# A branch on TensorE per step in a mixture-of-experts stage: 192 or 128 slots per expert

## The chip, the core and the metric

The kernel runs on one core of one Trainium2 chip. Its time is the device time of one execution in microseconds (us). TensorE multiplies matrices out of SBUF into PSUM, and each of its matmuls needs a weight load of its own; ScalarE (ACT in the rows), VectorE (DVE) and GpSimd (POOL) work on tiles; SyncE (SP) issues most transfers. Each engine has its own program and waits for the others through semaphores.

## The reference

Three stages follow each other: a sparse attention, a dense feed-forward layer with SiLU, and a routed layer with eight experts. Only the last is touched here:

```python
logits = x @ w_gate                      # x: 1152 tokens x 512
expert_idx = np.argmax(logits, axis=1)   # one expert per token
...
for i in range(N):                       # token i takes the next slot of its expert
    e = expert_idx[i]
    if counts[e] < capacity:             # capacity 288
        disp[e, counts[e]] = x[i]
        ...
h = np.maximum(np.einsum('ecd,edf->ecf', disp, w1), 0.0)   # 512 -> 1024, relu
y = np.einsum('ecf,efd->ecd', h, w2)                       # 1024 -> 512
out[i] = gate_w[i] * y[expert_idx[i], pos[i]]
```

How many tokens an expert gets depends on the data. With the inputs that `setup_inputs()` draws by default (seed 0), the reference's own counts are 138, 114, 113, 171, 190, 182, 128 and 116 tokens for experts 0 to 7.

## The kernel before

Attention and the feed-forward layer fill the first part of the program; the change leaves them as they are, except for eight more columns in the table of constants. Near the end of the feed-forward layer the tokens are routed: for every expert the kernel makes lists of its tokens in slots (`idx_g` to gather, `idx_o` to scatter, `gate`), with an index out of bounds in a slot that has no token.

The expert stage gives every expert NW = 192 slots, as a first chunk of P = 128 and a second of N1 = 64. Slots beyond 192 (up to the capacity) are done in a second pass at the end, which all engines skip if no expert needs it (`tc.If(flags[0] > 0)`, L1132). `r_final` counts the tokens of each expert by a matmul with ones, compares with 192 and writes the number of experts above it to `flag_i`; `get_flags` (L1087) loads it into a register of each engine, in the first step of expert 3.

The work of one expert is eight steps i, each for 128 of the 1024 hidden columns. In step (e, i) TensorE does
- `up` (L1055): four fp32 matmuls over the four blocks of 128 input columns, 192 slots wide, into a PSUM bank `u` (three banks in turn). In the trace each has two weight loads and two matmuls, so eight of each a step.
- `down` (L1074 to L1077 and `mm3`, L161 to L163) for the step three earlier (LAG = 3): five matmuls of 512 columns in fp32r. Three go into bank `y` (the first 128 slots), two into bank `z` (the 64 others).

Behind that come the step's other jobs (`fills`): ScalarE and VectorE split w2 of the next expert into a high and a low part (L235, L236, steps 0, 2, 4 and 6), TensorE turns the next expert's gathered tokens (`prep`, L930, steps 5 and 6), SyncE loads w1 and w2 of later experts. Then `relu` (L1061 on ScalarE, L1063 on VectorE) makes the tile `ht` of this step, which `down` takes three steps later; the bank `u` is free again at the same moment. After an expert's last `down`, `put_out` weighs both chunks with the gate and scatters them (L1044 to L1048); slots without a token are dropped by the bounds check.

Each engine runs its program in the order written; TensorE's order in the stage is up(s), down(s - 3), transposes if any, up(s + 1). Nothing reorders it.

Of the kernel before, what the change touches and what calls it, by code (L numbers as in the profile page):

```python
# [1 line left out]

# [7 lines left out]
F32 = mybir.dt.float32  # L10
F32R = mybir.dt.float32r
I32 = mybir.dt.int32
# [3 lines left out]
ALU = mybir.AluOpType  # L16
AX = mybir.AxisListType

P = 128
# [5 lines left out]
PW = 384  # L25
N1 = 64
NW = P + N1
# [12 lines left out]
LAG = 3  # L40
# [2 lines left out]
_C = {}  # L43
_off = 0
for _name, _w in (("ident", 128), ("ml", KW), ("ml0", KW), ("ms", 54), ("tri", 128),
                  ("rev", 8), ("tok", 18), ("iota", PW)):
    _C[_name] = (_off, _w)
    _off += _w
CW = _off
# [3 lines left out]
def constants():  # L53
    c = np.zeros((P, CW), np.float32)

    def put(name, a):
        o, w = _C[name]
        c[: a.shape[0], o:o + w] = a

    i = np.arange(P)  # L60
    put("ident", np.eye(P))
    q = (i % QB)[:, None]
    col = np.arange(KW)[None, :]
    ok = (col > q) & (col <= q + STRIDE)
    put("ml", np.where(ok, 0.0, -8e9))
    put("ml0", np.where(ok & (col >= STRIDE), 0.0, -8e9))
    c54 = np.arange(54)[None, :]
    ok = (q // 18 == c54 // 18) & (c54 % 18 <= q % 18)
    put("ms", np.where(ok, 0.0, -8e9))
    put("tri", (i[:, None] < i[None, :]) * 1.0)  # L70
    put("rev", np.broadcast_to(8.0 - np.arange(8), (P, 8)))
    tok = np.empty((P, 9, 2))
    tok[:, :, 0] = i[:, None]
    tok[:, :, 1] = P * np.arange(9)[None, :]
    put("tok", tok.reshape(P, 18))
    slot = np.full(PW, -1.0)
    slot[0:NW] = np.arange(NW)
    slot[2 * P:PW - 32] = NW + np.arange(P - 32)
    put("iota", np.broadcast_to(slot, (P, PW)))
    return c  # L80
# [3 lines left out]
def tile_kernel(ctx, tc, cap, q, k, v, w_in, w_out, w_gate, w1, w2, consts, out):  # L84
    nc = tc.nc
# [3 lines left out]
    E, _, F = w1.shape  # L89
# [8 lines left out]
    cst = ctx.enter_context(tc.tile_pool(name="cst", bufs=1))  # L98
    dram = ctx.enter_context(tc.tile_pool(name="dram", bufs=1, space=bass.MemoryType.DRAM))
    rp = ctx.enter_context(tc.tile_pool(name="rp", bufs=3))  # L100
# [11 lines left out]
    def C(name):  # L112
        o, w = _C[name]
        return cs[:, o:o + w]
# [7 lines left out]
    idx_g = cst.tile([P, 3, E], I32, name="idx_g")  # L122
    idx_o = cst.tile([P, 3, E], I32, name="idx_o")
    gate = cst.tile([P, 3, E], F32, name="gate")
    flag_i = cst.tile([1, 1], I32, name="flag_i")
    x2d = dram.tile([NT, DM], F32, name="x2d")

    pp = ctx.enter_context(tc.tile_pool(name="ps", bufs=1, space=bass.MemoryType.PSUM))
# [5 lines left out]
    def psum(tag):  # L134
        name = rings[tag].pop(0)
        rings[tag].append(name)
        return pp.tile([P, 512], F32, tag=name, name=tag, bufs=1)
# [22 lines left out]
    def mm3(o, ah, al, bh, bl, first, last):  # L160
        nc.tensor.matmul(o, lhsT=ah, rhs=bh, start=first, stop=False)  # L161
        nc.tensor.matmul(o, lhsT=ah, rhs=bl, start=False, stop=False)  # L162
        nc.tensor.matmul(o, lhsT=al, rhs=bh, start=False, stop=last)  # L163
# [82 lines left out]
    def l1_mm(g, tb, c, tag):  # L246
        s, o = 2 * (g % 2), P * c
        hp = psum(tag)
        for kk in range(KC):
            mm3(hp[:, 0:TB], whi[s][:, kk, o:o + P], wlo[s][:, kk, o:o + P],  # L250
                xhi[:, kk, tb * TB:(tb + 1) * TB], xlo[:, kk, tb * TB:(tb + 1) * TB], kk == 0, kk == KC - 1)
            if kk < KC - 1:
                yield
        yield hp[:, 0:TB]
# [35 lines left out]
    def first_up():  # L290
        for c in range(2):
            for hp in l1_mm(0, 0, c, "f"):
                if hp is not None:
                    copies.append((nc.vector.tensor_copy if c else nc.scalar.copy, hb[c], hp))
                yield


    with ExitStack() as actx:
# [212 lines left out]
        up = first_up()  # L511
# [21 lines left out]
        for i in range(NGR):  # L533
# [6 lines left out]
            n, part = groups[i][:2]  # L540
# [21 lines left out]
        z = NGR - VL  # L562
        up = l1_mm(0, 0, 2, "f")
        transpose_p(z + 1, "h")
        values(z)
        copy_out()
        normalise(z + 3, z - 1)
        next(up)
        transpose_p(z + 2)
        values(z + 1)  # L570
# [3 lines left out]
        silu(0, 0, 1, hb[1])  # L574
        evacuate_lo(z)
        next(up)
        next(up)
        transpose_p(z + 3, "h")
        hp = next(up)
# [7 lines left out]
        up = l1_mm(0, 0, 3, "acc")  # L587
# [205 lines left out]
    def r_slot_ids(out, src):  # L793
        t = rp.tile([P, 3, E], F32, tag="fin", name="fin", bufs=1)
        t = t[:, 0:src.shape[1], 0:src.shape[3]]
        nc.vector.scalar_tensor_tensor(out=t, in0=src[:, :, 0], scalar=-OOB, in1=src[:, :, 1],
                                       op0=ALU.mult, op1=ALU.add)
        nc.vector.tensor_scalar(out, t, OOB, None, op0=ALU.add)

    def r_final():  # L800
        extra = ohs
        cp = psum("m")
        for j, o in enumerate([cum] + extra):
            nc.tensor.matmul(cp[:, 0:E], lhsT=ones, rhs=o, start=j == 0, stop=j == len(extra))
        f = rp.tile([1, E], F32, name="flag", bufs=1)
        nc.vector.tensor_scalar(f, cp[0:1, 0:E], float(NW), None, op0=ALU.is_gt)
        fs = rp.tile([1, 1], F32, name="flags", bufs=1)
        nc.vector.tensor_reduce(out=fs, in_=f, axis=AX.X, op=ALU.add)
        nc.vector.tensor_copy(flag_i, fs)
        r_slot_ids(idx_o, idx)  # L810
# [69 lines left out]
    for n in range(4, nseq - 4):  # L880
        g, tb, c = seq[n]
# [167 lines left out]
            out=out, out_offset=bass.IndirectOffsetOnAxis(ap=idx_o[:n, ch, e:e + 1], axis=0), in_=y[:n], in_offset=None,  # L1049
            bounds_check=NT - 1, oob_is_err=False)  # L1050

    def up(e, i, n=NW):
        hp = psum("u")
        for kk in range(KC):
            nc.tensor.matmul(hp[:, 0:n], lhsT=w1b[e % 3][:, kk, P * i:P * i + P], rhs=X[e % 2][:, kk, 0:n],  # L1055
                             start=kk == 0, stop=kk == KC - 1)
        return hp

    def relu(hp, parts, n=NW):
        t = ep.tile([P, 2 * NW], F32R, tag="ht", name="ht", bufs=LAG + 1)  # L1060
        nc.scalar.activation(out=t[:, 0:n], in_=hp[:, 0:n], func=AF.Relu)  # L1061
        for o, c, m in parts:
            nc.vector.scalar_tensor_tensor(out=t[:, o:o + m], in0=hp[:, c:c + m], scalar=0.0, in1=t[:, c:c + m],  # L1063
                                           op0=ALU.max, op1=ALU.subtract)
        return t

    def down(e, i, t, y0, y1):
        j, c = 2 * (e % 2) + i // 4, i % 4
        for y in ((y1, y0) if i == 7 else (y0, y1)):
            if y is y0:  # L1070
                mm3(y0, t[:, 0:P], t[:, 2 * P:3 * P], whi[j][:, c], wlo[j][:, c], i == 0, i == 7)
            else:
                if i < 7:
                    nc.tensor.matmul(y1, lhsT=t[:, P:2 * P], rhs=whi[j][:, c], start=i == 0, stop=False)  # L1074
                nc.tensor.matmul(y1[:N1], lhsT=t[:, P:NW], rhs=wlo[j][:, c], start=False, stop=False)
                if i == 7:
                    nc.tensor.matmul(y1, lhsT=t[:, P:2 * P], rhs=whi[j][:, c], start=False, stop=True)  # L1077
# [6 lines left out]
    flags = []  # L1084

    def get_flags():
        flags.append(nc.values_load(flag_i[0:1, 0:1], min_val=0, max_val=E))  # L1087

    fills = {}

    def fill(e, i, *fs):
        fills.setdefault((e, i), []).extend(fs)

    fill(0, 0, (r_match, BB))
    fill(0, 1, (r_index, BA))
    fill(0, 2, (r_index, BB), (gather, 1, 0), (gather, 1, 1), (r_final,))
    fill(0, 3, (r_weigh, BA))
    fill(0, 4, (r_weigh, BB))
    for e in range(E):
        fill(e, 3 if e == 0 else 0, (gather, e + 2, 0))  # L1100
        fill(e, 4 if e == 0 else 1, (gather, e + 2, 1))
        for h in range(4):
            fill(e, SPLIT_AT[h], (split, e + 1, h))
        fill(e, 5, (prep, e + 1, 0))
        fill(e, 6, (prep, e + 1, 1))
        for j in range(2):
            fill(e, 3 + 4 * j, (w1load, e + 3, j))
    fill(3, 0, (get_flags,))

    r_match(BA)  # L1110
    PARTS = ((NW, P, N1), (NW + N1, 0, P))
    ht, ys = {}, {}
    for s in range(8 * E + LAG):
        e, i = divmod(s, 8)
        if s < 8 * E:
            hp = up(e, i)
        d, c = divmod(s - LAG, 8)
        if s >= LAG:
            if c == 0:
                ys[d] = psum("y"), psum("z")  # L1120
            down(d, c, ht.pop((d, c)), *ys[d])
        for f, *args in fills.pop((e, i), []):
            f(*args)
        if s < 8 * E:
            ht[e, i] = relu(hp, PARTS)
        if s >= LAG and c == 7:
            y0, y1 = ys.pop(d)
            put_out(d, 1, y1)
            put_out(d, 0, y0)
    assert not fills, fills  # L1130

    with tc.If(flags[0] > 0):  # L1132
        n = ROWS[2]
        for e in range(E):
# [11 lines left out]
            for i in range(8):  # L1146
                t = relu(up(e, i, n), ((n, 0, n),), n)
                j, c = 2 * (e % 2) + i // 4, i % 4
# [32 lines left out]
```

## Time and profile before

| | us |
|---|---|
| three runs | 485.38, 490.08, 487.12 (median 487.12) |
| the profiled execution, its own time | 483.33 |
| span of the trace in it | 481.5 |
| expert stage, first to last matmul | 303.5 to 470.3 |
| from there to the end of the span | 11.2 |

The span is the time from the first to the last instruction in the trace; 1.8 us of the execution's time lie outside it. The rows further down name an engine, a line of the kernel, the operation, and the tiles as out<-in. PE stands for TensorE's matmuls, PEld for its weight loads, and a q behind an engine's name for what its sequencer does itself: waits, register loads, branches. The matmul's times overlap with the next one's, so its cost is the distance from one start to the next.

### The profile page before, as it was taken

How to read it: one execution, taken by the hardware profiler on the slowest of the kernel's cores; microseconds unless marked ns; L12 is line 12 of the kernel's file. 1: busy time of each engine (PE TensorE's matmuls, PEld its weight loads, DVE VectorE, ACT ScalarE, POOL GpSimd, SP SyncE). 2: the span in 40 equal slices, each digit the busy share in tenths (PEclk: the TensorE clock that was granted, in tenths of full speed). 3: DMA queues.
4: the chain of work that ended last, by engine and by line, in shares of the span. 5: the costliest groups of instructions: out<-in, count | busy, mean ns of one | idle time of the engine just before them, and what ended most of it. 6: DMA issues, size and time to landing. Idle time of an engine off the chain costs nothing. (4 is left out here: it accounts for less than half of the span.)

```text
span 481.5 us, 8430 instructions
## 1 busy us (share of the span) xinstructions
PE 455.1 (95%) x3053; PEld 390.3 (81%) x3055; DVE 285.5 (59%) x785; ACT 203.8 (42%) x521; POOL 120.5 (25%) x152
## 2 busy tenths in 40 slices
PE   8989898999998989999999999999999999999990
PEld 4667677898887879887998888988888888888880
DVE  3676999357878855787325686654454454455210
ACT  4576787245463432534244143323343342423211
POOL 1323553012332320323054215420220303101001
PEclk9987999999999999999999999799999999999996
DMA  7989747014243650446034013998767677200000
GB/s 158 217 211 231 179 144 241 29 44 132 87 132 96 211 176 0 138 169 219 0 88 152 3 67 114 372 305 286 244 200 225 232 247 232 76 1 31 1 23 24
DMA packets 52363, 69.04 MB, mean 143 GB/s; under 512 B 19800, under 2 KB 29272, under 8 KB 52316
## 3 DMA queue, kind: packets, MB, share of 16 engines
q1 hardware_dynamic: 50268, 63.18, 42.8%
q0 software_dynamic: 2048, 5.26, 3.6%
q8 instruction: 26, 0.43, 0.4%
q14 instruction: 21, 0.17, 0.1%
HBM read 61.60 MB, written 7.86 MB: 144 GB/s over the span
## 5 line engine op out<-in xcount | busy, mean ns | idle before, releaser
L1055 PE MATMUL u<-X,w1b 128*128 128x192 f32 x512 | 95.7, 331 | 0.0
L1055 PEld LDWEIGHTS u<-X,w1b 128*128 128x128 f32 x512 | 86.1, 192 | 6.3
L198 POOL TENSOR_TENSOR wlo<-w,whi 128x512 fp32r<-128x512 f32 x32 | 44.2, 1383 | 117.4 <-DVE gl L267 79.5
L1061 ACT ACTIVATE ht<-u 128x192 fp32r<-128x192 f32 x64 | 21.2, 331 | 105.0 <-PE u L1055 65.2
L161 PE MATMUL acc<-whi,gh 128*128 128x512 f32 x144 | 58.2, 404 | 4.7 <-DVE x L288 4.6
L161 PE MATMUL h<-xhi,whi 128*128 128x384 f32 x176 | 59.8, 340 | 0.0
L163 PE MATMUL h<-xhi,wlo 128*128 128x384 f32 x176 | 59.4, 338 | 0.0
L162 PE MATMUL h<-xlo,whi 128*128 128x384 f32 x176 | 59.4, 338 | 0.0
L163 PE MATMUL acc<-whi,gl 128*128 128x512 f32 x144 | 56.9, 395 | 0.0
L162 PE MATMUL acc<-wlo,gh 128*128 128x512 f32 x144 | 56.7, 394 | 0.0
L1063 DVE SCALAR_TENSOR_TENSOR ht<-u,ht 128x64 fp32r<-128x64 f32 (+1 forms) x128 | 26.9, 252 | 46.7 <-ACT ht L1061 46.7
L266 ACT CAST gh<-g 128x384 fp32r<-128x384 f32 x48 | 24.6, 513 | 63.0 <-DVE g L259 63.0
L1048 POOL DMA_INDIRECT out_dram<-y,idx_o x16 | 15.5, 966 | 124.1 <-DVE y L1045 81.7
L259 DVE TENSOR_TENSOR g<-h,g 128x384 f32<-128x384 f32 x44 | 24.4, 554 | 35.5 <-ACT g L258 35.5
L267 DVE TENSOR_TENSOR gl<-g,gh 128x384 fp32r<-128x384 f32 x48 | 26.7, 557 | 25.7 <-ACT gh L266 25.5
L258 ACT ACTIVATE g<-h 128x384 f32<-128x384 f32 x44 | 21.5, 488 | 48.4 <-PE h L163 48.2
L189 DVE SCALAR_TENSOR_TENSOR wsb<-raw,wsb 128x512 uint32<-128x512 uint32 x32 | 39.3, 1228 | 1.0
L236 DVE TENSOR_TENSOR wlo<-raw,whi 128x1024 fp32r<-128x1024 f32 x28 | 34.2, 1222 | 9.2 <-ACT whi L235 9.2
L419 ACT ACTIVATE pr<-sc,st 128x54 f32<-128x54 f32 (+1 forms) x84 | 28.8, 344 | 17.6 <-DVE st L416 17.6
L161 PEld LDWEIGHTS acc<-whi,gh 128*128 128x128 f32 x144 | 27.0, 188 | 10.0 <-ACT w L186 5.5
L161 PEld LDWEIGHTS h<-xhi,whi 128*128 128x128 f32 x176 | 33.1, 188 | 1.9
L162 PEld LDWEIGHTS h<-xlo,whi 128*128 128x128 f32 x176 | 33.1, 188 | 1.8
(198 smaller groups left out, 854.7 us busy)
## 6 DMA issues: line engine op xcount, KB each, us to landing
w1b<-in_moe_w_dram SPq DMA_DIRECT2D x32, 512.0 KB
raw<-in_moe_w_dram SPq DMA_DIRECT2D x32, 512.0 KB
raw<-in_moe_w_in_dram SPq DMA_DIRECT2D x16, 512.0 KB
raw<-in_moe_w_out_dram SPq DMA_DIRECT2D x16, 512.0 KB
out_dram<-zw SPq DMA_DIRECT2D x1, 2304.0 KB
x2d<-x SPq DMA_DIRECT2D x2, 768.0 KB
vl<-in_v_dram SPq DMA_DIRECT2D x4, 288.0 KB
kr<-in_k_dram SPq DMA_DIRECT2D x4, 288.0 KB
```

Of the source, the lines that this page charges most:

```text
L161: nc.tensor.matmul(o, lhsT=ah, rhs=bh, start=first, stop=False)
L162: nc.tensor.matmul(o, lhsT=ah, rhs=bl, start=False, stop=False)
L163: nc.tensor.matmul(o, lhsT=al, rhs=bh, start=False, stop=last)
L189: nc.vector.scalar_tensor_tensor(out=u, in0=top, scalar=0x80000000, in1=u, op0=ALU.bitwise_and, op1=ALU.bitwise_or)
L198: nc.gpsimd.tensor_sub(wlo[slot][:, k], t, whi[slot][:, k])
L236: (nc.vector if e else nc.gpsimd).tensor_sub(wlo[slot][:, k], raw, whi[slot][:, k])
L259: nc.vector.tensor_mul(a, h, a)
L266: nc.scalar.copy(gh, a)
L267: nc.vector.tensor_sub(gl, a, gh)
L419: nc.scalar.activation(out=pr[:, a], in_=sc[:, a], func=AF.Exp, scale=-1.0, bias=st[:, 0, a:a + 1], accum_out=st[:, 1, a:a + 1])
L1055: nc.tensor.matmul(hp[:, 0:n], lhsT=w1b[e % 3][:, kk, P * i:P * i + P], rhs=X[e % 2][:, kk, 0:n], start=kk == 0, stop=kk == KC - 1)
L1063: nc.vector.scalar_tensor_tensor(out=t[:, o:o + m], in0=hp[:, c:c + m], scalar=0.0, in1=t[:, c:c + m], op0=ALU.max, op1=ALU.subtract)
```

## The change

`r_final` now compares the counts with two limits, 128 and 192, and multiplies each yes with a power of two, so that `flag_i` holds two bit masks with one bit per expert. The second mask takes the place of the old number in front of the second pass. The first is loaded into a register of TensorE alone (`get_wides`, step (0, 5)). From expert 1 on, TensorE's part of every step stands in an if and an else (`either`): with more than 128 tokens as before, else with `up` 128 columns wide and `down` without its two matmuls into `z`. Where up and down belong to different experts (three steps at each border) each has its own if and else. Expert 0 always runs 192 wide. ScalarE, VectorE, GpSimd and SyncE do in each step what they did, for 192 slots; each passes a jump to the next piece of the program where TensorE has its if and else, 77 of them. Bank `z` is one tile for all experts now, and the three banks `u` are three tiles in turn.

```diff
+                  ("rev", 8), ("bit", 8), ("tok", 18), ("iota", PW)):
...
+    put("bit", np.broadcast_to(2.0 ** np.arange(8), (P, 8)))
...
-        nc.vector.tensor_scalar(f, cp[0:1, 0:E], float(NW), None, op0=ALU.is_gt)
+        for j in range(2):
+            nc.vector.scalar_tensor_tensor(out=f[:, j], in0=cp[0:1, 0:E], scalar=float((P, NW)[j]), in1=C("bit")[0:1],
+                                           op0=ALU.is_gt, op1=ALU.mult)
...
-    def down(e, i, t, y0, y1):
+    def down(e, i, t, y0, y1, more=True):
...
-            else:
+            elif more:
...
+    def get_wides():
+        wides.append(nc.tensor.value_load(flag_i[0:1, 0:1], min_val=0, max_val=2 ** E - 1))
+
+    def either(e):
+        if e == 0:
+            yield 1
+        else:
+            with tc.If((wides[0] & (1 << e)) > 0) as cmp:
+                yield 1
+            with cmp.Else():
+                yield 0
...
+    fill(0, 5, (get_wides,))
...
-            hp = up(e, i)
-        d, c = divmod(s - LAG, 8)
+            hp = next(us)
         if s >= LAG:
             if c == 0:
-                ys[d] = psum("y"), psum("z")
-            down(d, c, ht.pop((d, c)), *ys[d])
+                ys[d] = psum("y"), y1
+            t = ht.pop((d, c))
+        for which in ((e,) if e == d else (e, d)):
+            for case in either(which) if 0 <= which < E else ():
+                if which == e:
+                    up(e, i, NW if case else P, hp)
+                if which == d:
+                    down(d, c, t, *ys[d], more=case)
```

An ordinary step on TensorE before (expert 1, `down` of the same expert; X and w1b are inputs of `up`, ht, whi and wlo those of `down`):

```order
L1055 MATMUL u<-X_3335,w1b_1520 128x192 x4
L161 MATMUL y<-whi_1515,ht 128x512
L162 MATMUL y<-wlo_1516,ht 128x512
L163 MATMUL y<-whi_1515,ht 128x512
L1074 MATMUL z<-whi_1515,ht 128x512
L1075 MATMUL z<-wlo_1516,ht 64x512
```

And with the change, from the branch to the last matmul of the else part:

```order
L1102 COMPARE_AND_BRANCH
L1059 MATMUL u<-X_3335,w1b_1520 128x192 x4
L163 MATMUL y<-whi_1515,ht 128x512
L164 MATMUL y<-wlo_1516,ht 128x512
L165 MATMUL y<-whi_1515,ht 128x512
L1078 MATMUL z<-whi_1515,ht 128x512
L1079 MATMUL z<-wlo_1516,ht 64x512
L1102 UNCONDITIONAL_BRANCH
L1059 MATMUL u<-X_3335,w1b_1520 128x128 x4
L163 MATMUL y<-whi_1515,ht 128x512
L164 MATMUL y<-wlo_1516,ht 128x512
L165 MATMUL y<-whi_1515,ht 128x512
```

The step stands twice now, one after the other. In front of the branch is one register operation, behind the else part a second jump, and each part begins with the wait for `relu` of three steps before.

TensorE at an expert's border with the change (first step of expert 2, with `down` of expert 1 behind it):

```order
L1102 REGISTER_ALU
L1102 COMPARE_AND_BRANCH
L1059 MATMUL u<-X_3334,w1b_3660 128x192 x4
L1102 UNCONDITIONAL_BRANCH
L1059 MATMUL u<-X_3334,w1b_3660 128x128 x4
L1102 UNCONDITIONAL_BRANCH
L1102 REGISTER_ALU
L1102 COMPARE_AND_BRANCH
```

Here `up` has its own if and else, and a second branch for `down` follows at once.

## Rows read from the trace of the kernel before

**Rows 1.** Busy time by stretch: length, engines' busy us, PE clock, DMA share, GB/s
```profile
343.70:364.40 20.70, 20.70 (x113) 18.15 (x112) 9.86 (x23) 7.76 (x15) 3.86 (x4) 1.00 0.73 235
470.30:481.50 11.20, 0.00 (x0) 0.00 (x0) 0.74 (x1) 0.69 (x1) 1.90 (x2) 0.62 0.07 26
```

**Rows 2.** PE in order of time, one step: start, us, then what
```profile
385.08 1.46 PE L1055 MATMUL u<-X,w1b 128*128 128x192 f32 x8
386.25 0.53 PE L161 MATMUL y<-whi,ht 128*128 128x512 f32 x1
386.61 0.39 PE L162 MATMUL y<-wlo,ht 128*128 128x512 f32 x1
386.83 0.39 PE L163 MATMUL y<-whi,ht 128*128 128x512 f32 x1
387.06 0.40 PE L1074 MATMUL z<-whi,ht 128*128 128x512 f32 x1
387.30 0.39 PE L1075 MATMUL z<-wlo,ht 128*64 128x512 f32 x1
387.53 0.32 PE L1055 MATMUL u<-X,w1b 128*128 128x192 f32 x1
```

**Rows 3.** PE groups of bank z, 300 to 482 us: count, busy us, mean ns
```profile
L1075 PE MATMUL z<-wlo,ht 128*64 128x512 f32 x64 | 25.8, 406 | 0.0
L1074 PE MATMUL z<-whi,ht 128*128 128x512 f32 x56 | 22.2, 396 | 0.0
L1077 PE MATMUL z<-whi,ht 128*128 128x512 f32 x8 | 3.1, 388 | 0.0
```

**Rows 4.** PEld and PE in order of time: fp32 work with fewer columns
```profile
292.02 0.86 PEld L652 LDWEIGHTS h<-wg,xt 128*128 128x128 f32 x7
...
358.51 0.60 PE L930 MATMUL m<-cs,xg 128*128 128x128 f32 x4
358.94 0.33 PE L1055 MATMUL u<-X,w1b 128*128 128x192 f32 x1
```

**Rows 5.** DMA queue q0, second scatter of experts 0, 1, 3, 6: packets, MB
```profile
q0 software_dynamic: 48, 0.02, 8.2%
...
q0 software_dynamic: 48, 0.00, 2.7%
...
q0 software_dynamic: 48, 0.09, 16.3%
...
q0 software_dynamic: 48, 0.00, 4.7%
```

**Rows 6.** Sequencers: ns min/median/max, first and last start (L1055 from 361.3 to 362.6)
```profile
L1055 PEldq EVENT_SEMAPHORE  x1: 946/946/946, 361.5 to 361.5; - x1
...
L1087 PEldq TENSOR_LOAD <-flag_i x1: 482/482/482, 363.3 to 363.3; - x1
```

**Rows 7.** PE in order of time: the matmuls right behind L1087, and the last one
```profile
366.88 1.46 PE L1055 MATMUL u<-X,w1b 128*128 128x192 f32 x8
...
469.86 0.39 PE L163 MATMUL y<-whi,ht 128*128 128x512 f32 x1
```

**Rows 8.** L1132, the branch over the second pass, on four sequencers (columns as Rows 6)
```profile
L1132 PEldq COMPARE_BRANCH  x1: 3771/3771/3771, 466.6 to 466.6; - x1
L1132 ACTq COMPARE_BRANCH  x1: 50/50/50, 470.3 to 470.3; - x1
L1132 DVEq COMPARE_BRANCH  x1: 72/72/72, 470.3 to 470.3; - x1
...
L1132 DVEq EVENT_SEMAPHORE  x1: 21/21/21, 471.1 to 471.1; - x1
...
L1132 POOLq COMPARE_BRANCH  x1: 45/45/45, 474.0 to 474.0; - x1
...
L1132 POOLq EVENT_SEMAPHORE  x5: 17/43/43, 474.5 to 477.0; - x5
```

**Rows 9.** DMA queue of TensorE's instructions, 466.58 to 470.35 us: packets, MB
```profile
q8 instruction: 1, 0.02, 1.7%
```

More of the change, by code (lines that the diff above doesn't have):

```diff
@@ L1 @@
+import itertools
 from contextlib import ExitStack
@@ L45 @@
 for _name, _w in (("ident", 128), ("ml", KW), ("ml0", KW), ("ms", 54), ("tri", 128),
-                  ("rev", 8), ("tok", 18), ("iota", PW)):
+                  ("rev", 8), ("bit", 8), ("tok", 18), ("iota", PW)):
     _C[_name] = (_off, _w)
@@ L124, in tile_kernel @@
     gate = cst.tile([P, 3, E], F32, name="gate")
-    flag_i = cst.tile([1, 1], I32, name="flag_i")
+    flag_i = cst.tile([1, 2], I32, name="flag_i")
     x2d = dram.tile([NT, DM], F32, name="x2d")
@@ L804, in r_final @@
             nc.tensor.matmul(cp[:, 0:E], lhsT=ones, rhs=o, start=j == 0, stop=j == len(extra))
-        f = rp.tile([1, E], F32, name="flag", bufs=1)
-        nc.vector.tensor_scalar(f, cp[0:1, 0:E], float(NW), None, op0=ALU.is_gt)
-        fs = rp.tile([1, 1], F32, name="flags", bufs=1)
+        f = rp.tile([1, 2, E], F32, name="flag", bufs=1)
+        for j in range(2):
+            nc.vector.scalar_tensor_tensor(out=f[:, j], in0=cp[0:1, 0:E], scalar=float((P, NW)[j]), in1=C("bit")[0:1],
+                                           op0=ALU.is_gt, op1=ALU.mult)
+        fs = rp.tile([1, 2], F32, name="flags", bufs=1)
         nc.vector.tensor_reduce(out=fs, in_=f, axis=AX.X, op=ALU.add)
@@ L1050, in put_out, with up @@
             bounds_check=NT - 1, oob_is_err=False)
-    def up(e, i, n=NW):
-        hp = psum("u")
+    def up(e, i, n=NW, hp=None):
+        hp = next(us) if hp is None else hp
         for kk in range(KC):
@@ L1086, in get_flags @@
     def get_flags():
-        flags.append(nc.values_load(flag_i[0:1, 0:1], min_val=0, max_val=E))
+        flags.append(nc.values_load(flag_i[0:1, 1:2], min_val=0, max_val=2 ** E - 1))
+    wides = []
+    def get_wides():
[8 more added lines that the diff above has]
+                yield 0
     fills = {}
@@ L1111, in tile_kernel @@
     PARTS = ((NW, P, N1), (NW + N1, 0, P))
-    ht, ys = {}, {}
+    ht, ys, y1 = {}, {}, psum("z")
+    us = itertools.cycle([psum("u") for _ in range(3)])
     for s in range(8 * E + LAG):
         e, i = divmod(s, 8)
+        d, c = divmod(s - LAG, 8)
         if s < 8 * E:
-            hp = up(e, i)
-        d, c = divmod(s - LAG, 8)
+            hp = next(us)
         if s >= LAG:
             if c == 0:
-                ys[d] = psum("y"), psum("z")
-            down(d, c, ht.pop((d, c)), *ys[d])
+                ys[d] = psum("y"), y1
[6 more added lines that the diff above has]
+                    down(d, c, t, *ys[d], more=case)
         for f, *args in fills.pop((e, i), []):
```

## The prediction

> **What bounds the kernel now.** I read the table of busy time by stretch first. [...] So TensorE sets the pace of the expert stage, and what it is spared there should shorten the kernel. After its last matmul 11.2 us follow, in which it does nothing [rows 1]; they stay.
>
> The order of time gives the price of each part of a step [rows 2]. From `up` to the next `up` it is 387.53 - 385.08 = 2.45 us. The two matmuls into `z` take 387.53 - 387.06 = 0.47. The five matmuls of 512 columns come every 0.23 us (386.61, 386.83, 387.06, 387.30, 387.53). The eight matmuls of `up` are 1.46 us long from the first start to the last end, so they start (1.46 - 0.33) / 7 = 0.161 us apart (0.33 is the length of one, [rows 4]); eight make 1.29.
>
> **Which experts become narrow.** The counts of the reference say 1, 2, 6 and 7 (114, 113, 128, 116 tokens); expert 0 is fixed as wide. Expert 6 lies on the limit, since the comparison is "greater than 128". The trace says the same. A second scatter has 48 packets, of which those for empty slots carry next to nothing: it moves 0.02 and 0.09 MB for experts 0 and 3, and 0.00 for 1 and 6 [rows 5]. So no token of expert 6 had a slot above 128 in this execution either.
>
> **What it removes.** Four narrow experts of eight steps make 32 `up` and 32 `down`.
> - `z`: 0.47 us x 32 = 15.0 us. The counts agree: 64 + 56 + 8 = 128 matmuls in 64 steps, two a step [rows 3].
> - `up`, 128 instead of 192 columns wide. No row shows this form. By columns alone it would be 0.161 x 128 / 192 = 0.107, and the fp32 transposes of 128 columns do start (358.94 - 358.51) / 4 = 0.108 us apart [rows 4]. But each matmul needs its weights, and where the fp32 matmuls are only 24 columns wide, the weight loads set the pace: seven span 0.86 us, (0.86 - 0.19) / 6 = 0.112 apart, 0.19 being the usual length of one [rows 4]. The bounds are 0.107 and 0.161 (no gain, if loads and matmuls stopped overlapping). I take 0.112, the larger of the two paces that must both be kept: 8 x (0.161 - 0.112) = 0.39 us a step, 12.5 in all.
>
> Together 27.5 us; a narrow step is then 2.45 - 0.47 - 0.39 = 1.59 us.
>
> **Who is late next in a narrow step.** VectorE has 9.86 us of work in an expert that then lasts 20.7 - 8 x 0.86 = 13.8; ScalarE 7.76. DMA moves 235 GB/s x 20.7 us = 4.9 MB an expert [rows 1]; in 13.8 us that is 353 GB/s, more than the 322 that a share of 1.00 would give at this rate. But w1 and w2 are ordered two to three experts before their use, only two narrow experts follow each other before wide ones, and 6 and 7 have their weights long before. The shortest chain is that of the next expert's tokens: transposed in steps 5 and 6, copied by VectorE behind a split, taken by the next `up`. I charge 0.5 us for it in all, and 0.2 for the tail, where the scatter of the empty chunk waits for the first of the last three matmuls instead of the last into `z`.
>
> **What it adds.** Each of the 77 branches is a register operation, a compare and, on either way, a jump or two. `get_wides` is a register load, 0.48 us long on TensorE [rows 6], before expert 1. All of it runs on the sequencer, and the question is how far that is ahead. The register load of L1087 stands right in front of the `up` that starts at 366.88, yet ran at 363.3 [rows 6, 7]: 3.6 us ahead, with 33 weight loads and matmuls queued between, and no gap followed in the matmuls. The branch at the end stands behind the matmul of 469.86 and began at 466.6 [rows 7, 8]. The sequencer is also quick: a wait held it from 361.5 for 0.946 us, and from its end at 362.45 to 363.3 it passed one whole step, 26 records in 0.85 us, at most 0.033 us each [rows 6]. A narrow step has 22 records: 0.73 us, with 0.05 for its wait and 0.1 for register operation and compare (compares take 0.045 to 0.072 on the other sequencers, [rows 8]). That leaves 1.59 - 0.88 = 0.71 us for the two jumps. The register load hides behind the queue.
>
> The price J of a jump of some 30 instructions is not shown. From below: 0, if it costs what other sequencer work does. From above: GpSimd goes on 474.5 - 474.0 = 0.5 us after its branch, 0.45 after its end, and VectorE 0.8 us after its own, part of it a wait for its own last work [rows 8]. TensorE's own branch took 3.77 us, and one page of its instructions came in during it [rows 8, 9]: that branch goes over the whole second pass. I take J below 0.2 us, the end at which nothing is fetched, and the branches then cost nothing that shows. [...]
>
> The jumps on the other four engines fall between work that fills half of their time. VectorE's one more operation in `r_final` is one on eight elements.
>
> **Sum.** 27.5 - 0.5 - 0.2 = 26.8 us less. Against the profiled execution that is 483.33 - 26.8 = 456.5; it lies 3.8 us under the median of the runs, 487.12, and from the median I get 460.3. I predict 460, the forecast's own range being 455 to 463.
>
> **Rivals.**
> - *The sequencer becomes the bound in part.* With J between 0.2 and 0.5 us the steps at the borders run over: a step with two branches has 4 J + 0.2 + 0.05 + 0.73 = 1.78 us at J = 0.2, against 1.59. Going through all steps with these prices, the loss is 1.3 us at 0.2, 5.7 at 0.3, 19 at 0.45, and 27.5, the whole gain, at 0.52. Times 461 to 485. GpSimd's row speaks for it, though other things can be in that half microsecond. Chance 0.12.
> - *The branch empties TensorE.* The long branch ended at 466.6 + 3.77 = 470.35, and the last matmul, by its length, at 469.86 + 0.39 = 470.25 [rows 7, 8]. If the compare waits until the array is done, each of the 77 costs the overlap of the last matmul (0.39 - 0.23 = 0.16), 0.10 until the branch ends, 0.05 for a wait and 0.19 for a weight load in the open: 0.50 us, 38.5 in all, 11 more than is gained: 498, slower. It decides from 27.5 / 77 = 0.36 us a branch on. Against it: the page was fetched during the branch, so its target was known before the end, and branches on ScalarE and VectorE are 0.05 and 0.07 us long with work still running behind them [rows 8]. Chance 0.12.
> - *Jumps of more than 0.52 us, or fetches at some of them* (VectorE's 0.7, TensorE's 3.77): over 487, slower. Chance 0.03.
> - *It does not do what it says for expert 6*, whose 128 tokens become 129 by a tie: 6.9 us less gain, 467. Against it is its scatter [rows 5]. Chance 0.04.
> - *The forecast*, chance 0.69.
>
> **Numbers.** About 1% is what a measurement of this kernel tells from no change; the bounds are 482.3 and 492.0. Faster has the forecast, expert 6 and nearly all of the first rival: 0.84. Within 1% is the end of the first rival and a cheap emptying: 0.03. Slower: 0.13. The range is 454 (no charge for chain and tail, less a microsecond for the median) to 477, which takes in two thirds of the first rival and leaves out 0.19.
>
> **What would show it.** In the trace of the changed kernel the narrow experts should take about 13.8 us and the wide ones 20.7; matmuls of `up` 0.112 apart in the first; no `z` in them; TensorE without idle time at a branch and its branches 2 us and more ahead of the matmuls behind them. Gaps of half a microsecond at every branch would show the emptying; gaps at the borders alone, the sequencer; more pages on the instruction queue than the longer program has, the fetches. The forecast is wrong if narrow experts take more than 15 us.

## The result, and the profile after

The changed kernel takes 459.4 us, the median of four runs (455.49 to 461.34); the kernel before took 486.25, the median of four runs (479.49 to 490.08). The ratio is 0.951, with a 95% interval of 0.936 to 0.966: faster. The ratios here go by the fast runs alone, since some runs of a kernel are slower by a per cent or two, so a ratio isn't that of the medians. Run a second time, the changed kernel gave 0.953 (0.948 to 0.958). The profiled execution fell from 483.33 to 455.49 us, by 27.8; its span fell from 481.5 to 453.6.

The busy time by stretch comes first, as in [rows 1]: length, then what PE, PEld, DVE, ACT and POOL are busy, the granted clock, the DMA share and GB/s. The stretches are narrow expert 2, wide expert 4, and what follows the last matmul:

```profile
336.20:349.91 13.71, 13.71 (x97) 12.29 (x96) 9.34 (x24) 7.54 (x15) 3.36 (x3) 1.00 1.00 353
369.19:389.81 20.62, 20.62 (x113) 18.14 (x112) 9.76 (x24) 7.75 (x15) 3.85 (x4) 1.00 0.79 253
440.49:453.60 13.11, 0.00 (x0) 0.00 (x0) 0.74 (x1) 0.96 (x2) 1.90 (x2) 0.70 0.06 22
```

A narrow expert lasts 13.71 us and TensorE is busy in all of it; a wide one keeps its 20.6. The DMA engines are at 1.00 in the narrow one and move the 353 GB/s that the same weights need in less time. The tail grew from the 11.2 us of [rows 1] to 13.1.

TensorE in order of time, two narrow steps, answers to [rows 2]: start, us, then what.

```profile
337.78 1.05 PE L1059 MATMUL u<-X,w1b 128*128 128x128 f32 x8
338.59 0.47 PE L163 MATMUL y<-whi,ht 128*128 128x512 f32 x1
338.91 0.39 PE L164 MATMUL y<-wlo,ht 128*128 128x512 f32 x1
339.14 0.40 PE L165 MATMUL y<-whi,ht 128*128 128x512 f32 x1
339.37 1.05 PE L1059 MATMUL u<-X,w1b 128*128 128x128 f32 x8
340.18 0.47 PE L163 MATMUL y<-whi,ht 128*128 128x512 f32 x1
```

From `up` to `up` it is 339.37 - 337.78 = 1.59 us. The eight matmuls of `up` give way to `y` after 338.59 - 337.78 = 0.81 us, where 192 columns took 386.25 - 385.08 = 1.17 [rows 2]. Nothing stands between L165 and the next `up`, and there is no idle time at a branch.

The groups of TensorE by shape, 300 us to the end, answer to [rows 3]: count, busy us, mean ns, idle us before them.

```profile
L1059 PE MATMUL u<-X,w1b 128*128 128x192 f32 x256 | 47.5, 329 | 0.0
L1059 PE MATMUL u<-X,w1b 128*128 128x128 f32 x256 | 34.0, 276 | 0.0
...
L1079 PE MATMUL z<-wlo,ht 128*64 128x512 f32 x32 | 13.0, 406 | 0.0
L1078 PE MATMUL z<-whi,ht 128*128 128x512 f32 x28 | 11.0, 393 | 0.0
...
L1081 PE MATMUL z<-whi,ht 128*128 128x512 f32 x4 | 1.6, 391 | 0.0
```

Half of everything: 256 of 512 matmuls of `up` are 128 wide, and 32 + 28 + 4 = 64 matmuls into `z` are left of 128. So four experts went the narrow way, expert 6 with its 128 tokens among them.

The branches on TensorE's sequencer (ns min/median/max, first and last start). Both the compare and the jump over the else part are called COMPARE_BRANCH there:

```profile
L1102 PEldq COMPARE_BRANCH  x110: 67/179/426, 318.3 to 437.2; - x110
L1102 PEldq ALU_OP  x77: 36/36/42, 318.2 to 437.1; - x77
```

77 register operations, 77 compares, and 33 jumps over the else part in the wide experts. A compare that goes on into the if part takes 67 to 77 ns, one that goes to the else part mostly 208 to 222, a jump mostly 169 to 179; twelve of the 110 take longer, 0.25 to 0.43 us. The second jump, behind the else part, leaves no record. The first compare starts at 318.3, the `up` that it stands before at 321.10: 2.8 us ahead.

At the end the last matmul answers to [rows 7], in TensorE's order of time:

```profile
440.10 0.39 PE L165 MATMUL y<-whi,ht 128*128 128x512 f32 x1
```

The branch over the second pass answers to [rows 8], here that of TensorE:

```profile
L1158 PEldq COMPARE_BRANCH  x1: 3802/3802/3802, 438.6 to 438.6; - x1
```

GpSimd's waits and scatters from 436 us on (of the two waits the first, 2867 ns, belongs to the last scatter of expert 6, the second to the scatter of expert 7's empty chunk):

```profile
L1052 POOLq EVENT_SEMAPHORE  x2: 2867/3486/4105, 434.6 to 441.7; - x2
L1052 POOL DMA_INDIRECT out_dram<-y,idx_o x2: 912/948/985, 441.8 to 446.5; - x2
```

The last matmul ends at 440.49, the long branch at 438.64 + 3.80 = 442.44, two microseconds later. It doesn't end with the array's work, as it seemed to in [rows 8]. And GpSimd waits 4.1 us between its two last scatters. In the kernel before, from 470 us on, it waited 2.3:

```profile
L1048 POOLq EVENT_SEMAPHORE  x1: 2317/2317/2317, 471.2 to 471.2; - x1
```

That is where the tail grew.

Where did the 27.9 us of the span come from? The trace can be cut at the first `up` of expert 1, before which nothing was changed but `r_final`, one register load and the eight columns of constants. This is where that `up` starts before:

```profile
323.09 1.30 PE L1055 MATMUL u<-X,w1b 128*128 128x192 f32 x7
```

And after:

```profile
321.10 1.06 PE L1059 MATMUL u<-X,w1b 128*128 128x128 f32 x8
```

From there to the last matmul's start it was 469.86 - 323.09 = 146.77 us before and is 440.10 - 321.10 = 119.00 now, 27.77 less. The tail takes back 1.9. The remaining 2.0 us came before expert 1 (at 321.10 instead of 323.09) and can't be put down to the change: in the other traces below, that moment lies anywhere from 320.3 to 326.8.

### The profile page after: what moved, and what is told of

Same layout as the page of the kernel before. It is cut to its first block, busy times and chain, and to the rows that moved or that the text cites. A ratio compares the mean times of both kernels' runs of the same rounds, so it can differ in the third digit from the quotient of the medians.

```text
span 453.6 us, 8533 instructions
## 1 busy us (share of the span) xinstructions
PE 426.3 (94%) x2991; PEld 365.9 (81%) x2991; DVE 284.4 (63%) x786; ACT 203.4 (45%) x521; POOL 121.6 (27%) x152
## 5 line engine op out<-in xcount | busy, mean ns | idle before, releaser
L1059 PE MATMUL u<-X,w1b 128*128 128x192 f32 (+1 forms) x512 | 81.5, 302 | 0.0
L1059 PEld LDWEIGHTS u<-X,w1b 128*128 128x128 f32 x512 | 75.2, 190 | 5.2
L165 PE MATMUL h<-xhi,wlo 128*128 128x384 f32 x176 | 59.5, 338 | 0.0
L165 PE MATMUL acc<-whi,gl 128*128 128x512 f32 x144 | 56.7, 394 | 0.0
L269 DVE TENSOR_TENSOR gl<-g,gh 128x384 fp32r<-128x384 f32 x48 | 26.8, 558 | 25.6 <-ACT gh L268 25.5
L421 ACT ACTIVATE pr<-sc,st 128x54 f32<-128x54 f32 (+1 forms) x84 | 28.8, 345 | 18.4 <-DVE st L418 18.4
```

The lines of the kernel that those rows point to most:

```text
L269: nc.vector.tensor_sub(gl, a, gh)
L421: nc.scalar.activation(out=pr[:, a], in_=sc[:, a], func=AF.Exp, scale=-1.0, bias=st[:, 0, a:a + 1], accum_out=st[:, 1, a:a + 1])
```

## The experiments

My theory: the branches run on TensorE's sequencer while the array works, and cost nothing; the gain is that of the spared matmuls, the narrow `up` being paced by its weight loads. Rivals: a branch empties the array; the sequencer becomes the bound at the borders. Stretches are given from the first `up` of expert 1 to the start of the last matmul unless other ends are named, since the part ahead varies by some microseconds from execution to execution.

### The same matmuls without a branch

```diff
-        if e == 0:
-            yield 1
-        else:
-            with tc.If((wides[0] & (1 << e)) > 0) as cmp:
-                yield 1
-            with cmp.Else():
-                yield 0
+        yield e in (0, 3, 4, 5)
...
-    fill(0, 5, (get_wides,))
```

> The choice is written into the program: experts 1, 2, 6 and 7 narrow, the others wide, with no register, branch or second copy of a step, so the kernel holds for these counts alone. TensorE has the same matmuls to do as in the changed kernel. If the branches are free, as I think, the stage from the first up to the last matmul stays at 137.4 us (the changed kernel's trace: 302.69 to 440.10), narrow expert 2 at 13.7 and wide expert 4 at 20.6, and the time is that of the changed kernel, 459 +- 3. If each of the 77 branches emptied TensorE (0.50 us each), it is 38 us less: 421. If the sequencer were the bound at the borders alone, border steps fall from 2.05 and 1.99 us and 1 to 6 us are gained: 453 to 458. The two microseconds more behind the last matmul (13.1 instead of 11.2): gone, if they come of the longer program; still there, if they come of expert 7 being narrow.

457.15 us (455.99 to 458.83), ratio 0.945 (0.940 to 0.950). The stretch goes from the first of these matmuls to the second:

```profile
326.80 1.06 PE L1059 MATMUL u<-X,w1b 128*128 128x128 f32 x8
...
445.80 0.39 PE L165 MATMUL y<-whi,ht 128*128 128x512 f32 x1
```

That is 445.80 - 326.80 = 119.00 us, the 119.00 of the changed kernel. Experts 2 and 4:

```profile
341.89:355.61 13.72, 13.72 (x97) 12.29 (x96) 9.39 (x24) 7.64 (x15) 4.28 (x5) 1.00 0.95 351
374.89:395.51 20.62, 20.62 (x113) 18.14 (x112) 9.93 (x23) 7.77 (x15) 3.86 (x4) 1.00 0.73 248
```

In this stretch all 77 branches together cost less than 0.1 us. The emptying and the sequencer at the borders are both out. (From the first `up` of expert 0, the 137.4 of the expectation, it was 138.2; the difference is expert 0's, which lasted 18.4 us in the one trace and 19.2 in the other.) The median lies 2 us under the changed kernel's, and the trace of this kernel has a tail of 10.3 us instead of 13.1: the two microseconds more are gone without the longer program, though expert 7 is narrow here too. The last experiments are about that.

### All branches, nothing spared

```diff
-                    up(e, i, NW if case else P, hp)
+                    up(e, i, NW, hp)
...
-                    down(d, c, t, *ys[d], more=case)
+                    down(d, c, t, *ys[d])
```

> All 77 branches stay, but the else part does what the if part does: 192 columns and both matmuls into z. Nothing is spared, so what the time is above that of the kernel before is the price of branches alone. Free branches: the stage takes 166.3 us as before (303.53 to 469.86), every expert 20.65, and the time is 486 +- 3. Branches that empty TensorE: 38 us more, 524. Sequencer as the bound: no step should show it here, since two branches (0.56 us by the records of the changed kernel) and 26 records of at most 0.033 us make 1.4 us against a step of 2.45.

485.54 us, ratio 1.003 (0.9997 to 1.0065). The stretch:

```profile
324.64 1.47 PE L1059 MATMUL u<-X,w1b 128*128 128x192 f32 x8
...
471.38 0.39 PE L165 MATMUL y<-whi,ht 128*128 128x512 f32 x1
```

It is 471.38 - 324.64 = 146.74 us against 146.77 before. Expert 2, which takes the else part:

```profile
345.28:365.94 20.66, 20.66 (x114) 18.15 (x113) 9.86 (x23) 7.76 (x15) 4.32 (x4) 1.00 0.68 237
```

The same test from the other side, with the same answer.

### Each half of the gain alone

```diff
-                    up(e, i, NW if case else P, hp)
+                    up(e, i, NW, hp)
```

> The else part leaves out the two matmuls into z, but up stays 192 columns wide. By the rows it saves 0.47 us a step: ordinary narrow steps 1.98 us, expert 2 16.9 instead of 20.7, 15.0 us in all, so a time near 471. If the two parts of the gain weren't independent (the weight loads being the bound of the whole step), it would save less than 0.47 a step here or less than 0.39 in the other half.

```diff
-                    down(d, c, t, *ys[d], more=case)
+                    down(d, c, t, *ys[d])
```

> The else part does up 128 columns wide, but both matmuls into z. By the pace of the weight loads it saves 8 x (0.161 - 0.112) = 0.39 us a step: ordinary narrow steps 2.06 us, expert 2 17.6 us, 12.5 us in all, so a time near 474. By columns alone (0.107) it would be 0.43 a step and 2.02.

Busy time of expert 2 with `z` left out, in the first of the two kernels:

```profile
343.82:360.79 16.97, 16.97 (x98) 15.54 (x96) 9.59 (x24) 7.76 (x15) 4.35 (x4) 1.00 0.87 288
```

And with the narrow `up` alone, in the second:

```profile
340.22:357.62 17.40, 17.40 (x114) 14.91 (x112) 9.59 (x23) 7.77 (x15) 4.49 (x4) 1.00 0.80 280
```

The stretch is 457.47 - 325.48 = 131.99 us without `z`, 14.8 less than before, and 456.54 - 322.83 = 133.71 with the narrow `up`, 13.1 less. Together 27.84, and both at once gave 27.77: the two are independent. (Single executions took 472.58 and 470.01 us.)

### `up` only 64 columns wide

```diff
-                    up(e, i, NW if case else P, hp)
+                    up(e, i, NW if case else 64, hp)
```

> In the else part up is 64 columns wide instead of 128; the tokens in slots 64 to 127 of experts 1, 2, 6 and 7 are left out of it. If the 128 x 128 weight loads set the pace of a narrow up (0.112 us each), nothing more is gained: matmuls of up still 0.112 apart, ordinary narrow steps 1.59 us, expert 2 13.7 us, time as the changed kernel, 459 +- 3. If columns set it, they come 0.054 apart and a step loses another 0.47 us: 1.12, expert 2 10.0 us, 15 us less, 444 (or a little more, if VectorE with 9.9 us of work an expert is next).

TensorE in order of time, one step:

```profile
345.33 1.00 PE L1059 MATMUL u<-X,w1b 128*128 128x64 f32 x8
346.14 0.47 PE L163 MATMUL y<-whi,ht 128*128 128x512 f32 x1
...
346.92 1.00 PE L1059 MATMUL u<-X,w1b 128*128 128x64 f32 x8
```

A step is 346.92 - 345.33 = 1.59 us, as with 128 columns, and `y` follows `up` after the same 0.81; only the last matmul itself is shorter (1.00 instead of 1.05 from first start to last end). 459.1 us in a single execution. So the columns don't set the pace any more, as forecast, and 128 is as narrow as it pays to go. That it is the weight loads that do, and not some shortest distance between fp32 matmuls, is borne out by the trace of the kernel before, where four transposes of 64 columns have weights of 64 rows instead of 128:

```profile
382.13 0.46 PE L930 MATMUL m<-cs,xg 64*128 64x64 f32 x4
```

At 0.235 us each in the mean they start (0.46 - 0.235) / 3 = 0.08 us apart, closer than the 0.112 of 64 columns with 128 rows of weights.

### Five branches a step, then three

```diff
-    def up(e, i, n=NW, hp=None):
+    def up(e, i, n=NW, hp=None, kks=range(KC)):
...
-        for which in ((e,) if e == d else (e, d)):
...
+        if s < 8 * E:
+            for kk in range(KC):
+                for case in either(e):
+                    up(e, i, NW if case else P, hp, (kk,))
+        if s >= LAG:
+            for case in either(d):
+                down(d, c, t, *ys[d], more=case)
```

> Five branches a step instead of one: each of the four matmuls of up in an if and an else of its own, and down in a fifth. The matmuls stay. By the records of the changed kernel a branch to the else part takes the sequencer 0.036 + 0.215 us, one through the if part 0.036 + 0.07 + 0.175. A narrow step then needs 5 x 0.25 + 22 x 0.033 + 0.05 = 2.0 us of the sequencer against 1.59 of the array: the sequencer becomes the bound, expert 2 takes about 16.5 us instead of 13.7, and the kernel loses about 11 us (470). A wide step needs 2.3 against 2.45 and stays, 20.6 an expert. If the records overlap with what the queue does anyhow, or 0.033 us is far too high a bound for a matmul's record, narrow steps stay near 1.6. If a branch emptied the array, a narrow step would grow by 4 x 0.5 us to 3.6.

474.34 us in a single execution; the stretch is 460.75 - 326.76 = 133.99, 15.0 more than with one branch a step. Busy time of experts 2 and 4:

```profile
341.88:359.60 17.72, 17.65 (x98) 13.97 (x97) 9.81 (x24) 7.79 (x15) 6.10 (x6) 1.00 0.86 290
381.73:403.12 21.39, 21.39 (x113) 17.90 (x112) 9.86 (x23) 7.77 (x15) 3.84 (x4) 1.00 0.72 232
```

TensorE's register operations, one a branch, from 340 to 360 us, about expert 2 (columns as above):

```profile
L1102 PEldq ALU_OP  x45: 36/36/36, 340.2 to 359.9; - x45
```

The same from 381 to 403 us, a wide stretch:

```profile
L1102 PEldq ALU_OP  x42: 36/36/36, 381.0 to 402.8; - x42
```

The sequencer is the bound here: in expert 2 a branch with what it holds comes every (359.9 - 340.2) / 44 = 0.45 us, in the wide stretch every (402.8 - 381.0) / 41 = 0.53. The direction was right, the size too small. Expert 2 came out at 17.7 us instead of 16.5, and wide experts grew by 0.8 to 2.9 us where I had expected nothing. I had added up lengths of records: for a branch of `up` with its four matmul records 0.251 + 4 x 0.033 = 0.38 us in a narrow step and 0.281 + 4 x 0.033 = 0.41 in a wide one. The distances from branch to branch below are 0.390 and 0.478, so it is in the wide steps above all that time between the records was missing. Between the matmuls of one narrow `up` (352.5 to 353.5 us) the distance can be read directly:

```profile
L1102 PEldq ALU_OP  x3: 36/36/36, 352.6 to 353.4; - x3
```

That is (353.4 - 352.6) / 2 = 0.4 us from branch to branch, 0.390 by the trace's finer starts, with two weight loads and two matmuls in between. Through the if part, in a wide step, three follow each other like this:

```profile
L1102 PEldq ALU_OP  x3: 36/36/36, 376.3 to 377.2; - x3
```

(377.2 - 376.3) / 2 = 0.45, by the finer starts 0.478.

PE's busy time hides this: 17.65 of 17.72 us, hardly any idle. The slow pace shows in TensorE's order of time, where eight matmuls of `up` that took 1.05 us now take 1.35:

```profile
352.89 1.35 PE L1059 MATMUL u<-X,w1b 128*128 128x128 f32 x8
354.23 0.50 PE L163 MATMUL y<-whi,ht 128*128 128x512 f32 x1
```

Expert 1, the first with branches, still took 15.1 us as in the changed kernel, and the loss began in expert 2: by my estimate a lead like the 2.8 us of the changed kernel's trace was used up first. With three branches a step (the edit against the kernel with five):

```diff
-            for kk in range(KC):
+            for kks in ((0, 1), (2, 3)):
...
-                    up(e, i, NW if case else P, hp, (kk,))
+                    up(e, i, NW if case else P, hp, kks)
```

> Three branches a step: two matmuls of up in each of two, down in the third. With five, a branch of up with its four records took the sequencer 0.390 us in a narrow step and 0.475 in a wide one, and whole steps 2.13 and 2.70. By that a narrow step needs 2 x 0.47 + 0.57 = 1.51 us here, just under the array's 1.59, and a wide one 2 x 0.55 + 0.80 = 1.9 against 2.45: every expert as in the changed kernel, expert 2 13.7 and expert 4 20.6 us, time 459 +- 3. If the price isn't additive in the branches (the fetch after a jump counting by the jump, not by the record), a narrow step is over 1.7 and expert 2 over 14.5.

459.18 us in a single execution, stretch 444.34 - 325.34 = 119.00, expert 2:

```profile
340.44:354.15 13.71, 13.71 (x97) 12.29 (x96) 9.29 (x24) 7.52 (x15) 3.42 (x3) 1.00 0.97 349
```

Three branches a step cost nothing that shows (119.00 us), five cost 15.0. The 1.51 us forecast from the distances measured with five agrees with that, but all that this run shows of the sequencer is that three branches need no more than the array's 1.59.

### The end: the second pass left out, and the empty scatter left out

```diff
-    fill(3, 0, (get_flags,))
...
-    with tc.If(flags[0] > 0):
-        n = ROWS[2]
...
-            put_out(e, 2, y2)
```

> The changed kernel without the second pass and the branch over it; for these counts the pass is skipped anyhow, so what is left out is code alone. In the changed kernel the empty scatter at the end was waited for 4.1 us, and a page of TensorE's instructions came in during that wait; in the kernel before no page came in during it, and the wait was 2.3. If the page of the far branch is what holds the scatter up, the wait is 2.2 to 2.5 us here and some 11.2 us or less follow the last matmul. If expert 7 being narrow does it, the wait stays at 3.4 to 4.1 us and 12.4 to 13.1 us follow. The stage stays at 137.4.

456.27 us in a single execution. GpSimd's waits and scatters at the end (the 2868 ns belong to the last scatter of expert 6):

```profile
L1052 POOLq EVENT_SEMAPHORE  x2: 2186/2527/2868, 441.5 to 446.8; - x2
L1052 POOL DMA_INDIRECT out_dram<-y,idx_o x2: 911/948/986, 446.9 to 449.7; - x2
```

Busy time behind the last matmul:

```profile
445.61:454.49 8.88, 0.00 (x0) 0.00 (x0) 0.74 (x1) 0.95 (x2) 1.90 (x2) 0.70 0.07 27
```

The wait is back at 2.2 us, though expert 7 is narrow. The transfers by queue (packets, MB, share) from the scatter's issue to the end of the wait, in the changed kernel, 441.81 to 445.76 us:

```profile
q8 instruction: 1, 0.02, 1.5%
q14 instruction: 2, 0.02, 1.5%
q0 software_dynamic: 48, 0.00, 0.6%
```

And here, 446.93 to 448.96 us:

```profile
q0 software_dynamic: 48, 0.00, 1.2%
```

The scatter's own 48 packets are the same; what differs is the page on TensorE's instruction queue q8 and the two packets on q14, of which the kernel before has one too, with its wait of 2.3 us. Over the traces the picture holds: where a q8 page started between the scatter's issue and its end (the changed kernel twice, `z` alone, 64 columns, three branches) the wait was 3.4 to 4.1 us; where none did (the kernel before, the narrow `up` alone, both parts alike, five branches) 2.2 to 2.5. In the kernel before a page was under way at the issue, from 471.13 to 472.19 us; it was over when the scatter's first packet started, at 472.82. The kernel without branches, with 2.9 and no q8 page, lies between. So neither the narrow expert nor the second pass's code by itself makes the wait long: five branches have both, and wait 2.2 us.

That a page goes with late packets, this same trace shows at another place. Here a page came in behind the empty scatter of expert 6, which GpSimd issued at 437.09 us. The next scatter starts after an idle time of 3.61 us, where the changed kernel's had 1.91:

```profile
441.61 0.99 POOL L1052 DMA_INDIRECT out_dram<-y,idx_o  x1 [3.61 <-DMA out_dram<-y,idx_o]
```

Up to 439.30 us, while the page was still under way, the transfers of that scatter were:

```profile
q8 instruction: 1, 0.02, 3.1%
q0 software_dynamic: 45, 0.00, 1.0%
```

45 of the 48 packets had gone; the last three, of 4 or 8 bytes, start only at 439.77, when the page's 1.09 us are over. In the changed kernel's scatter of expert 7 it is the same: 45 packets by 444.60, the last three behind the page. They go 1.0 us later for it here, and 1.2 in the changed kernel; why the scatter's end then comes another 1.0 us after them, against 0.3 to 0.5 without a page, stays open. So what leaving out the second pass did away with is the page at expert 7's scatter. Of the 4.2 us by which this tail is shorter than the changed kernel's, 1.9 are that wait; the other 2.3 lie behind the last scatter, from whose start it is 7.1 us to the end there and 4.8 here.

The other way to be rid of the wait is to skip the scatter, on GpSimd alone, with the same bit:

```diff
-        nc.gpsimd.indirect_dma_start(
...
+        def scatter():
...
+        if (e, ch) == (E - 1, 1):
+            with tc.If((pools[0] & (1 << e)) > 0):
+                scatter()
+        else:
+            scatter()
...
+    fill(5, 5, (get_pools,))
```

> The changed kernel, with the last expert's scatter of the second chunk in an if of GpSimd alone (by the same bit): expert 7 has no token there. In the changed kernel's trace GpSimd issues that scatter at 441.8 us, then waits 4.1 us for it (2.3 in the kernel before), and issues the scatter of the first chunk at 446.5, from which 7.1 us lead to the end. Without it the last scatter can go as soon as ScalarE has its tile, 441.5: 4.5 us less in that trace, 2.7 if the usual wait is 2.3; time 455 to 457, ratio to the changed kernel about 0.99. If the 4 us are a transfer queue that is busy for another reason at that moment, the last scatter meets it instead and 2 us or less are left. If GpSimd's jump costs what the long one of TensorE does (3.8 us), nothing is gained.

457.18 us, ratio 0.940 (0.932 to 0.947); the six runs spread from 450.48 to 458.29. Run again, beside the changed kernel:

> The changed kernel once more, beside the next one on the same chip: 459 +- 2, ratio to the kernel before 0.945 to 0.952, stage 137.4 us.

> The kernel without the last expert's empty scatter once more, on the same chip as the changed kernel. In its first trace 9.4 us followed the last matmul, against 13.1 in the changed kernel's and 11.2 in that of the kernel before. If that holds in every execution it is 2 to 4 us faster than the changed kernel, some 0.6%; if the 13.1 was a chance of one execution, 1.5 to 2.

454.05 us, ratio 0.942 (0.936 to 0.948), beside 459.64, ratio 0.953 (0.948 to 0.958). GpSimd in order of time in the second trace, its last scatter:

```profile
440.90 0.98 POOL L1054 DMA_INDIRECT out_dram<-y,idx_o  x1 [5.69 <-ACT y L1051]
```

Busy time behind the last matmul:

```profile
439.64:449.68 10.04, 0.00 (x1) 0.00 (x0) 0.74 (x1) 0.96 (x2) 0.98 (x1) 0.71 0.08 29
```

One scatter is left, released by ScalarE, and 9.4 and 10.0 us follow the last matmul in the two traces, against 13.1 and 12.5 in the changed kernel's: 2.5 to 3.7 us are the skip's, where 2.7 to 4.5 were expected. From the start of the scatter that is left it is 8.1 and 8.8 us to the end, against 7.1 in the changed kernel: a q8 page comes in behind its issue in both traces, so part of the wait has moved to it. The medians lie 5.6 apart; what the tails don't explain is the part ahead of the stage (the first `up` at 301.84 in this trace, 306.14 in the other). It beats the kernel before by some 6%, and the changed kernel by about 0.6% as the traces' tails have it; the intervals of the two overlap a little, so that they differ isn't shown by the times alone.

## Why the prediction was right

Predicted were 460 us, 456.5 for the profiled execution; measured were 459.4 and 455.49. The sum was 26.8 us; the stage gave 27.77, and less the 1.9 of the tail 25.8 are left. That the times agree still better is in part luck. The 460 started from a median of 487.12, which lay above most other runs of the kernel before (medians 483.8 to 484.0 beside the experiments). By the ratios the change saves 4.9 and 4.7%, some 23.6 and 22.8 us of 483 (16 to 31 and 20 to 25 by their intervals), where stage and tail of the two traces give 25.8 and 26.5. In the second trace the difference lies ahead of expert 1, whose first `up` starts at 325.96 us instead of 323.09. Whether the change makes that part longer isn't shown: there is one trace of the kernel before, and among the others the moment varies from 320.3 to 326.8.

- **What bounds the stage.** TensorE, busy for 20.70 of 20.70 us in [rows 1]. Everything spared on it shortened the kernel (14.8 us for `z` alone, 13.1 for the narrow `up`), and the granted clock was 1.00 in both kinds of expert.
- **Removing `z`.** Forecast 15.0 us, measured 14.8 alone.
- **The narrow `up`.** Forecast 12.5 us, measured 13.1. The pace of 0.112 us from the weight loads was right (1.59 us a step, and 64 columns gain nothing more). A step gained 0.41 us instead of 0.39. In the order of time 0.36 of it lies before the first matmul into `y` and 0.04 behind that one, which is followed after 338.91 - 338.59 = 0.32 us instead of 386.61 - 386.25 = 0.36 [rows 2]: seven of the sum's eight distances lie in the first piece, the eighth in the second.
- **The chain of the next tokens,** 0.5 us: not paid. Expert 2's steps with transposes take no longer than the narrow steps and the transposes themselves. The DMA engines are at 1.00 in that expert and nobody on TensorE waited for them. The 322 GB/s that I had put down for a share of 1.00 wasn't a ceiling: 353 were moved at that share.
- **The length of a narrow expert.** Forecast 13.8 us, and over 15 was to be a sign of being wrong. Expert 2 took 13.71, but experts 1 and 6 took 15.10: in their first three steps `down` still belongs to a wide expert, with `z`, 3 x 0.47 = 1.4 us. Wide expert 3 is shorter by as much, 19.28. The sign hadn't taken the borders into account; the mechanism holds.
- **The tail,** 0.2 us: mis-sized. It grew by 1.9 in the profiled execution and by 1.3 in the second trace of the changed kernel. I had followed the empty scatter to its issue, not to its end. The issue came 441.81 - 440.49 = 1.32 us after the last matmul instead of 471.33 - 470.25 = 1.08, the 0.2 of the sum; the wait behind it went from 2.3 to 4.1 us. By chance about the same was given back ahead of expert 1.
- **The branches.** Forecast free, with a jump under 0.2 us, which was my estimate. Measured: 0.390 us a branch to the else part with four records, at most 0.033 us each, and 0.1 for register operation and compare; that leaves 0.16 to 0.29 for the two jumps. The break-even of 0.52 a jump was far off. The sequencer was, however, not always 2 us ahead. At step 4 of each wide expert its branch came 0.6, 0.9 or 1.0 us before the `up` behind it, since the wait for bank `z` stands in the if part of step 3. In expert 3 VectorE had just weighed the `z` of expert 2; the wait (L1078) ended at 357.3, the matmul ran on time at 357.9, and only the lead had shrunk.
- **The emptying.** Its one support was that the long branch seemed to end with the array [rows 7, 8]. After, it ends 2 us later, without the second pass the last branch takes 0.2 us, and in the stage 77 branches cost nothing beside a program that has none.
- **Pages on the instruction queue.** 26 in the kernel before, by its queues:

```profile
q8 instruction: 26, 0.43, 0.4%
```

  And in the changed kernel:

```profile
q8 instruction: 32, 0.52, 0.5%
```

  Six pages more, 0.09 MB, while q14 has 21 in both. The kernel without branches, which has no second copy of a step, has 26 again, so the six are these copies. None of the 110 branch records is longer than 0.43 us, so none waited as the long one does, with its 3.80. While that one lasted, from 438.64 to 442.44 us, one q8 page came in, as in [rows 9]; which jumps need a page isn't shown.

## What to carry to other kernels

A branch on TensorE costs its sequencer some 0.3 us here (0.1 and the 0.16 to 0.29 above). The stage lost nothing by one or three of them in a step of 1.59 us, and 15.0 us by five: count the sequencer's time per step by the distance from record to record, not by their lengths, and compare it with the step. Before narrowing a matmul, look in the trace for the pace of its weight loads, 0.112 us here; 64 columns took the same 1.59 us a step as 128. When the main engine gets shorter, read the tail again, and look at transfers of instructions there as well as those of data.

## What was not expected of the hardware

- A compare that falls through takes 67 to 77 ns on TensorE's sequencer, one that jumps mostly 208 to 222, an unconditional jump mostly 169 to 179; on ScalarE, VectorE and GpSimd the branch at the end takes 45 to 72.
- A page of one engine's instructions goes with a longer wait for another engine's transfer: in five traces in which a page on TensorE's queue started between issue and end of a scatter without a single token, GpSimd waited 3.4 to 4.1 us for it, in five without one 2.2 to 2.5, and in a sixth 2.9.
- Without the second pass, which the changed kernel skips, it was 4.8 us from the last scatter's start to the end instead of 7.1, in a single execution.
- The stage repeats to 0.01 us: from the first `up` of expert 1 to the last matmul it was 119.00 us in both traces of the changed kernel, in both without the empty scatter, without the second pass, with three branches and with none. What varies lies ahead of it and behind it: in the traces it began between 320.3 and 326.8 us, and 8.9 to 13.1 us followed its end.
